# Attention decode with streamed K and V: a 31st chunk slot, smaller work tiles, and V as the stationary operand for more head pairs

## The chip, the cores and the metric

The kernel runs on one core of a Trainium2 chip. The metric is the device time of one launch in microseconds (us); three runs of the kernel before gave 1102.74, 1104.28 and 1105.88, so its median is 1104.28 us. A core has five engines that run their own instruction streams: TensorE (PE in the profile, with its weight loads shown as PEld), VectorE (DVE), ScalarE (ACT), GpSimd (POOL) and SyncE (SP). SP computes nothing here: it issues the DMAs. The engines wait for one another by semaphores.

## The reference

Two layers of the same two blocks run over 8 batch rows `b`, each with one query token: attention against a cache (A), then an MLP with two layer norms (B). Both layers read the same K and V caches, and 16 query heads share 8 K/V heads of 4096 positions by 256 elements in bf16.

```python
def _A_ref(x, k_cache, v_cache, wq, wo):
    q = (x @ wq).reshape(B, 1, 16, 256).transpose(0, 2, 1, 3)
    k = jnp.repeat(k_cache, 2, axis=1); v = jnp.repeat(v_cache, 2, axis=1)
    scores = jnp.einsum("bhqd,bhkd->bhqk", q, k) * (256 ** -0.5)
    o = jnp.einsum("bhqk,bhkd->bhqd", _softmax(scores), v)
    return o.transpose(0, 2, 1, 3).reshape(B, 1, 4096) @ wo
...
x = A_x
for _ in range(2):
    x = x + _A_ref(_layernorm(x), A_k_cache, A_v_cache, A_wq, A_wo)
    x = x + _B_ref(_layernorm(x), B_w1, B_w2, B_w3, B_w4)
```

`_B_ref` is, for one token, `x1 = x` (its shifted branch moves the only token out) followed by `x1 + gelu(layernorm(x1) @ w3) @ w4`. Rows of the batch don't mix, so one row can finish layer 0 and start layer 1 while the next row is still in layer 0.

## The kernel before

**Tiling.** The work is cut by batch row `b` and by pair `m` of K/V heads (0 to 3). A pair has two heads `s`, and a head's K (and V) is four chunks `c` of 128 partitions by 2048 elements, 0.524 MB each. A chunk lives in a slot of SBUF; there are `NSLOT = 30` slots, four to a slab. One DMA (line 444) loads one chunk, or two or four into adjacent slots that begin at a multiple of two or four (`run`, inside `schedule`); a group that finds no such run while the DMA queue is about to dry up is split in two.

**Scores.** K must be transposed first. For some chunks (`NN[m]` of each head: 1, 0, 1, 1) PE transposes into PSUM (line 810), ACT copies back (869), and PE multiplies (879). The others are transposed in blocks of 32 by DVE (891, about 1.2 us for half a chunk) from the raw slot into a second slot, and PE multiplies them (900) by a query laid out to match, in the tile `qe`. `diagonal` (602 to 633) makes that query: a DVE multiply (618), four matmuls (624), a DVE multiply (630). `qe` has two tiles, one a layer, each with room for four pairs, and one call of `diagonal` makes up to four pairs: 10 calls in layer 0 and 24 in layer 1. Softmax follows on DVE, POOL, ACT and PE (914 to 933) and leaves the probabilities in one of `NP = 4` tiles `pT` (some also in one of `NZ = 4` tiles `pN`). The tile is taken by `kpart` and given back by `vpart`.

**P*V.** `vpart` has two forms. With `still` V is the stationary operand: 16 matmuls a chunk with two moving columns (963), then a DVE reduction and multiply (966, 969). Without it p is stationary and V moves: 8 matmuls a chunk (990) into four groups of PSUM rows, which are then gathered: two ACT copies into the tile `half` (997), a matmul between them (1000), eight small matmuls (1006) and a DVE multiply (1010). Before, 17 of the 64 pairs (counting both layers and all rows) are `still`: the last pair of each row's layer 0, the first of the two pairs in each turn, and the very last pair.

**Two layers and the turn.** Row `b` runs layer 0 with all K and V streamed; pairs 1 to 3 of its K stay on chip (24 chunks, three of them parked in PSUM by `park` and put back by `unpark`, 1083). Then comes the `turn` (635 to 681): a chain of small operations that ends layer 0 (output projection 1034, `w3`, `gelu`, `w4` 587, layer norms), projects the query (`rows_`, 662), copies the rows by ACT into `qrow`, which is the tile `qe[0]` (666), transposes them (`columns`, 670) and makes layer 1's queries. During the turn SP loads V for the last pair of layer 0 and for pairs 2 and 3 of the previous row's layer 1. Then layer 1 runs on the K that stayed (pairs 1, 2, 3, no K loads), streams K of pair 0, and V; V of pairs 2 and 3 is used only in the next row's turn, so two `pT` tiles are held until then.

**Order.** The program lists all operations with priorities and costs; `Plan.schedule` plays them through a cost model and writes each engine's order. On the chip each engine runs its list in that order and waits by semaphore where an input, a buffer or a PSUM bank isn't free. SP's list is one order of loads, each of which waits for the last readers of its slot.

Of the kernel before, what the change touches and what calls it, by code (L numbers as in the profile page):

```python
# [3 lines left out]
P = 128  # L4
# [3 lines left out]
HKV = 8  # L8
# [4 lines left out]
NSLOT = 30  # L13
SLOT = 2048
AHEAD = (1, 2)
NT = 2
NS = 2
NV = 2
NP = 4
NN = (1, 0, 1, 1)  # L20
NZ = 4
# [3 lines left out]
STILL = (True, False)  # L25
# [329 lines left out]
def bass_interleave_layers__gqa_block_cached__mixer_s_mlp__decode_kernel(  # L355
# [37 lines left out]
    qe = [sb(f"qe{i}", [P, 512], bf) for i in range(2)]  # L393
    half = sb("half", [P, 1024], bf)
    pT = [sb(f"pT{i}", [P, P], bf) for i in range(NP)]
    pN = [sb(f"pN{i}", [P, 64], bf) for i in range(NZ)]

    qrow = qe[0]

    def pack(name, dt, sizes):  # L400
# [4 lines left out]
        "small32", f32, [5, 4, 4, 5, 5, 4, 8, 14, NP * 4, 8, NS * 16])  # L405
# [186 lines left out]
    Bqe = [[Buf() for _ in range(HKV // 2)] for _ in range(2)]  # L592

    def place(layer, b, m):


        return (1, b - 1) if layer == 0 and m == 0 and b in AHEAD else (layer, m)

# [3 lines left out]
    def diagonal(layer, b, m0=0, m1=4):  # L602

        k, p0 = place(layer, b, m0)
        p1 = p0 + m1 - m0
        n = 2 * (m1 - m0)
        c0 = 384 if layer else 256
        part = psT[:, c0 + 32 * m0:c0 + 32 * m1]  # L610
        qm = qe[k][:, 128 * p0:128 * p0 + 16 * n]
        bufs = [Bqe[k][m] for m in range(p0, p1)]

        def spread(e):
            src = psT[:, 64 + 8 * m0:64 + 8 * m1] if layer else qo[:, 8 * m0:8 * m1, b]
            o, i0, i1 = (qm.rearrange("p (q x) -> p q x", q=4), src.unsqueeze(1).to_broadcast([P, 4, 8 * (m1 - m0)]),
                         quarter.unsqueeze(2).to_broadcast([P, 4, 8 * (m1 - m0)]))
            return e.tensor_tensor(o, i0, i1, ALU.mult)
        dve(spread, 150 + 16 * n, [Bsel] + ([] if layer else [Bq1[b]]), bufs, [bT] if layer else [], name=f"q{layer}b{b}{m0}m")
# [7 lines left out]
        add("pe", emit, 140, bufs + [Bsel], [], [bT], name=f"q{layer}b{b}{m0}s")  # L627

        def put(e):
            return e.tensor_tensor(qe[k][:, 128 * p0:128 * p1].rearrange("p (n a h) -> p n a h", a=4, h=2),  # L630
                                   part.rearrange("p (n h) -> p n h", h=2).unsqueeze(2).to_broadcast([P, 8 * n, 4, 2]),
                                   quarter.unsqueeze(1).unsqueeze(3).to_broadcast([P, 8 * n, 4, 2]), ALU.mult)
        dve(put, 150 + 32 * n, [Bsel], bufs, [bT], name=f"q{layer}b{b}{m0}")

    def turn(b):
# [30 lines left out]
        add("act", lambda e: e.activation(qrow[:, :], psT[:, :], ACT.Copy, scale=sf[:, 2:3]), 590, [Bs["f"]], Bqe[0], [bT], name=n + "qr")  # L666

        def columns(e):
            for j in range(4):
                last = e.matmul(psT[:, 64:96].rearrange("p (r g j) -> p j r g", r=2, j=4)[:, j], qrow[:, P * j:P * j + P],  # L670
                                ident[:, :].rearrange("p (g r) -> p r g", g=4)[:, 0:2, :], start=True, stop=True)
            return last
        add("pe", columns, 300, Bqe[0] + [Bc], [], [bT], name=n + "qc", n=4)
        for ms in ((1,), (2, 3, 0)):
            if 0 in ms:
                dve(lambda e: e.tensor_copy(q2, psT[:, 64:96]), 180, [], [Bq2], [bT], name=n + "q2")
            for m in ([(1, 2)] if len(ms) == 1 else [(2, 4), (0, 1)]):
                diagonal(1, b, *m)
        plan.ops[-1].turn = "end"
        plan.turn, plan.prio = False, keep  # L680
        return ready
# [132 lines left out]
    def kpart(at, layer, b, m, kept, most=2):  # L814
# [34 lines left out]
        k, pm_ = place(layer, b, m)  # L849
        bq = Bq2 if layer else Bq1[b]  # L850
        for s in range(2):
            h = 2 * m + s
            for c in range(NCH):
# [32 lines left out]
                for t in range(2):  # L886
# [9 lines left out]
                    def score(e, u=u, c=c, t=t, s=s):  # L896
                        o = spot(psS[x])[:, :, c, t, :, s]
                        for g in range(8):
                            i = 1024 * t + g * P
                            last = e.matmul(o, slots[u.slot][:, i:i + P], qe[k][:, 128 * pm_ + 64 * s + 8 * g:128 * pm_ + 64 * s + 8 * g + 8],  # L900
# [155 lines left out]
    def K(layer, b, m, most=2):  # L1056
        at[0] += 1.0
        if layer == 0 and m < 2:
# [3 lines left out]
            elif m == 0:  # L1062
                diagonal(0, b)
# [223 lines left out]
```

## Time and profile before

| what | value |
|---|---|
| median of three runs | 1104.28 us (1102.74 to 1105.88) |
| the profiled execution | 1105.02 us, its span 1103.2 us |
| PE busy | 771.1 us, 17760 matmuls; 17807 weight loads |
| DVE busy | 746.4 us, 1417 instructions |
| ACT busy | 245.9 us |
| DMA | 446.80 MB on SP's queue, 98.2% of the 16 DMA engines' span |
| instruction loads by DMA | 139 packets, 2.28 MB |
| loads of 1, 2 and 4 chunks | 44, 218 and 88 (K and V) |
| 891, DVE transposes | 512 of 1214 ns, 598.7 us |
| 997, ACT copies into `half` | 94 of 602 ns, 56.6 us |
| 618 and 630, DVE, one pair | 192 and 289 ns |
| 630, DVE, four pairs in one | 685 ns |

A busy share is an average over stages. A row of the windows view gives, for a stretch of the span, each engine's busy time with the number of its instructions, the granted PE clock, the DMA engines' busy share and the rate in GB/s. A line of the chain of waits gives a start, a duration and the work that the end of the kernel was waiting for at that time; "issue" there is time in which PE waited for nothing that the profile shows.

### The profile page before, as it was taken

The page shows a single profiled execution, that of the slowest core. Times are in us where ns is not written, and L with a number is a line of the kernel's source. Part 1 is how long each engine was busy: PE and PEld are TensorE (multiplying, and loading weights), DVE is VectorE, ACT ScalarE, POOL GpSimd, SP SyncE. Part 2 cuts the span into 40 slices and gives each one's busy share as a digit, 9 for nine tenths or more (in the row PEclk, how much of TensorE's full clock was granted, in tenths as well). Part 3 has the DMA queues.
Part 4 walks back from the last instruction along what each step waited for, and adds up shares of the span by engine and source line. Part 5 has one row for each costly group of instructions (what it writes and reads, how often), then busy time and mean ns, then how long its engine had stood idle before and what let it go on. Part 6 is the DMA issues. An engine that isn't in the chain of part 4 may idle for free.

```text
span 1103.2 us, 38162 instructions
## 1 busy us (share of the span) xinstructions
PE 771.1 (70%) x17760; PEld 601.0 (54%) x17807; DVE 746.4 (68%) x1417; ACT 245.9 (22%) x352; POOL 69.9 (6%) x200
## 2 busy tenths in 40 slices
PE   2567576778667875778758787577766787577875
PEld 2355465466546563566536665456644566355654
DVE  3999447964696379855698458974589737885542
ACT  1033122122212131313212133121321214121310
POOL 0000001000100010000100000000000001000010
PEclk9997565565555555555555556555565556655555
DMA  9999999999999999999999999999999999999994
GB/s 348 406 420 405 396 405 409 423 408 403 425 422 411 405 427 427 422 396 417 423 425 421 401 403 426 427 418 404 416 424 424 412 405 427 425 421 400 421 423 169
DMA packets 57743, 449.24 MB, mean 407 GB/s; under 512 B 5856, under 2 KB 11888, under 8 KB 18032
## 3 DMA queue, kind: packets, MB, share of 16 engines
q1 hardware_dynamic: 57584, 446.80, 98.2%
q8 instruction: 139, 2.28, 0.8%
q14 instruction: 20, 0.16, 0.0%
HBM read 446.77 MB, written 0.01 MB: 405 GB/s over the span
## 4 chain that ended last, share of the span: by engine, by line
PE 30%; DMA 30%; DVE 23%; issue 9%; ACT 4%; POOL 0%; POOLq 0%; DVEq 0%
DMA slot<-in_A_k_cache_dram 19%; DVE slot L891 17%; DMA slot<-in_A_v_cache_dram 11%; PE psS L900 10%; PE psV L990 8%; PE psT L662 3%; ACT slot L1083 3%; PE psS L879 2%; PE psK L810 2%; PE psT L587 1%; PE psV L963 1%; ACT half L997 1%; PE psT L1034 1%; PE psT L624 1%; PE psV L1006 1%
## 5 line engine op out<-in xcount | busy, mean ns | idle before, releaser
L891 DVE STREAM_TRANSPOSE slot<-slot 128x1024 bf16<-128x1024 bf16 x512 | 598.7, 1214 | 40.3 <-DMA slot<-in_A_k_cache_dram 35.3
L900 PE MATMUL psS<-qe,slot 128*128 128x8 bf16 x6528 | 258.8, 175 | 164.5 <-DVE slot L891 121.7
L900 PEld LDWEIGHTS psS<-qe,slot 128*128 128x128 bf16 x6528 | 221.5, 104 | 236.5 <-DVE slot L891 165.7
L990 PE MATMUL psV<-slot,pT 128*2 128x256 bf16 x2448 | 154.3, 383 | 5.3 <-DMA slot<-in_A_v_cache_dram 3.6
L869 ACT COPY slot<-psK 128x1024 bf16<-128x1024 bf16 x112 | 110.8, 1027 | 168.6 <-PE psK L810 168.5
L997 ACT ACTIVATE half<-psV 128x512 bf16<-128x512 f32 x94 | 56.6, 602 | 345.6 <-PE psV L990 328.1
L810 PE MATMUL psK<-ident,slot 128*128 128x128 bf16 x896 | 104.5, 303 | 15.7 <-DMA slot<-in_A_k_cache_dram 8.1
L810 PEld LDWEIGHTS psK<-ident,slot 128*128 128x128 bf16 x896 | 88.2, 141 | 17.6 <-DMA slot<-in_A_k_cache_dram 8.8
L990 PEld LDWEIGHTS psV<-slot,pT 128*2 128x2 bf16 x2448 | 57.0, 100 | 30.5 <-issue 3.6
L914 DVE TENSOR_REDUCE small<-psS 128x4 f32<-128x128 f32 x64 | 18.4, 287 | 70.2 <-PE psS L900 69.8
L916 POOL PARTITION_ALL_REDUCE small<-small x64 | 23.9, 374 | 621.2 <-DVE small L914 621.2
L963 PE MATMUL psV<-pT,slot 128*128 128x2 bf16 x1632 | 54.2, 166 | 11.7 <-DMA slot<-in_A_v_cache_dram 11.3
L963 PEld LDWEIGHTS psV<-pT,slot 128*128 128x128 bf16 x1632 | 49.9, 105 | 20.5 <-DMA slot<-in_A_v_cache_dram 14.1
L879 PE MATMUL psS<-small,slot 128*128 128x2 bf16 x896 | 32.2, 166 | 25.8 <-issue 19.9
L879 PEld LDWEIGHTS psS<-small,slot 128*128 128x128 bf16 x896 | 28.2, 104 | 31.2 <-issue 20.6
L929 DVE STREAM_TRANSPOSE pT<-psS 128x128 bf16<-128x128 bf16 x64 | 19.2, 300 | 37.9 <-PE psS L927 37.7
L1034 PE MATMUL psT<-small,wo_sb 128*128 128x1 bf16 x1024 | 34.7, 165 | 8.1 <-DVE small L969 3.9
L921 ACT ACTIVATE pT<-psS 128x128 bf16<-128x128 f32 x64 | 18.2, 285 | 99.0 <-DVE psS L918 99.0
L932 POOL PARTITION_ALL_REDUCE small<-small x64 | 27.8, 435 | 185.0 <-DVE small L930 174.1
L879 PE MATMUL psS<-qo,slot 128*128 128x2 bf16 x768 | 28.0, 167 | 16.2 <-ACT slot L869 10.8
L990 PE MATMUL psV<-slot,pN 128*2 128x256 bf16 x560 | 38.4, 370 | 0.5 <-DMA slot<-in_A_v_cache_dram 0.4
L1034 PEld LDWEIGHTS psT<-small,wo_sb 128*128 128x128 bf16 x1024 | 30.9, 103 | 12.0 <-DVE small L1010 5.1
(148 smaller groups left out, 638.8 us busy)
## 6 DMA issues: line engine op xcount, KB each, us to landing
slot<-in_A_v_cache_dram SPq DMA_DIRECT2D x149, 1024.0 KB, 10.0
slot<-in_A_k_cache_dram SPq DMA_DIRECT2D x45, 2048.0 KB, 15.4
slot<-in_A_v_cache_dram SPq DMA_DIRECT2D x43, 2048.0 KB, 21.0
slot<-in_A_k_cache_dram SPq DMA_DIRECT2D x69, 1024.0 KB, 11.2
slot<-in_A_v_cache_dram SPq DMA_DIRECT2D x42, 512.0 KB, 6.5
wo_sb<-in_A_wo_dram SPq DMA_DIRECT2D x4, 896.0 KB, 19.2
wq_sb<-in_A_wq_dram SPq DMA_DIRECT2D x3, 1024.0 KB, 9.7
w_sb<-in_B_w_dram SPq DMA_DIRECT2D x1, 1568.0 KB, 16.4
```

The lines of the kernel that those rows point to most:

```text
L662: last = e.matmul(psT[32 * g:32 * g + 2, :], syn[:, 4 - r if k == 3 else k, 1 - r:3 - r], w, start=(r == 0 and k == 0), stop=(r == 1 and k ...
L810: last = e.transpose(tile[:, j * P:(j + 1) * P], slots[u.slot][:, o:o + P], ident[:, :])
L869: return e.copy(slots[u.slot][:, 1024 * t:1024 * t + 1024], tile)
L879: last = e.matmul(o, slots[u.slot][:, i:i + P], q, start=(cc == 0), stop=(cc == 1))
L891: return e.transpose(o, i)
L900: last = e.matmul(o, slots[u.slot][:, i:i + P], qe[k][:, 128 * pm_ + 64 * s + 8 * g:128 * pm_ + 64 * s + 8 * g + 8], start=(g == 0), stop= ...
L932: add("pool", lambda g: g.partition_all_reduce(db, rs, P, ReduceOp.add), 450, [B_["rs"]], [B_["db"]], prio=pr + 1, name=n + "db")
L963: last = e.matmul(o, slots[u.slot][:, i:i + P], w, start=(j == 0), stop=(j == 7))
L990: last = e.matmul(psV[x][32 * i:32 * i + 2, DH * s:DH * s + DH], w, slots[u.slot][:, DH * j:DH * j + DH], start=(c == 0 and k == 0), stop= ...
L997: add("act", lambda e, i=i: e.activation(part(i), psV[x][:, :], ACT.Copy, scale=1.0 if i else -1.0), 590, [], [Bhalf[i]], [bV[x]], prio=at ...
L1034: last = e.matmul(psT[:, 4 * (2 * s + i) + c:4 * (2 * s + i) + c + 1], wo_sb[:, a, d0:d0 + P], o1[b % 2][:, a:a + 1], start=(k == 0), stop ...
L1083: E = add("act", lambda e, v=v, t=t, tile=tile: e.copy(slots[v.slot][:, 1024 * t:1024 * t + 1024], tile), 1045, [], [], [bank], [v], prio= ...
```

## The change

It makes room for one more slot and changes how a few things are held:

- `NSLOT` is 31. The 31st slot is the third of its slab, so only single chunks can use it.
- `half` is gone. The gather of P*V (lines 985 to 1009) takes a free slot for its two copies, through the planner, from its first copy to its last small matmul.
- `qe` is one tile for a ring of two pairs. `diagonal` makes one pair a call; in the turn it is called for pairs 1 and 2 of layer 1, and all other calls come from `K`, just ahead of the pair's scores. A call reuses the place of the pair before last and so waits for that pair's scores.
- The query rows of the turn go into the slot in which a parked chunk's half is to be put back. That chunk's second half is put back before the copy, and its first half after `columns`.
- `NP` and `NZ` are 3. To keep that possible, `K` calls `V` of an earlier pair before it takes its own tile.
- Row sums share the statistics' columns with the maxima; the reciprocal's order after other DVE instructions is now a wait on DVE's own semaphore.
- `still` is set for both pairs in a turn, and for pair 2 of layer 0 in rows 1 to 7: 32 of the 64 pairs.

```diff
-NSLOT = 30
+NSLOT = 31
-NP = 4
+NP = 3
-NZ = 4
+NZ = 3
-STILL = (True, False)
...
-    qe = [sb(f"qe{i}", [P, 512], bf) for i in range(2)]
-    half = sb("half", [P, 1024], bf)
+    qe = sb("qe", [P, 256], bf)
...
+    def diagonal(layer, b, m):
+        k = nq[0] % 2
+        nq[0] += 1
+        qk = qe[:, 128 * k:128 * k + 128]
+        qm = qk[:, 0:32]
...
+        v, Brow = kept[b, 3][1, 0], Buf()
+        E = unpark(b, 1, ready, [1], -1.0)
+        R = add("act", lambda e: e.activation(slots[v.slot][:, 0:512], psT[:, :], ACT.Copy, scale=sf[:, 2:3]), 590, [Bs["f"]], [Brow], [bT], [v], name=n + "qr")
+        R.deps[E] = False
...
+        C = add("pe", columns, 300, [Brow, Bc], [], [bT], [v], name=n + "qc", n=4)
+        unpark(b, 1, C, [0], -0.4)
+        diagonals[1, b, 1] = diagonal(1, b, 1)
+        dve(lambda e: e.tensor_copy(q2, psT[:, 64:96]), 180, [], [Bq2], [bT], name=n + "q2")
+        diagonals[1, b, 2] = diagonal(1, b, 2)
...
-            part = lambda i: half[:, 512 * i:512 * i + 512]
+            v, Bhalf = Unit(f"{n}H", None, 0), [Buf(), Buf()]
+            part = lambda i: slots[v.slot][:, 512 * i:512 * i + 512]
...
+    def K(layer, b, m, most=2, after=None):
         at[0] += 1.0
+        prio = at[0]
+        if (layer, b, m) not in diagonals:
+            plan.prio = -0.9 if layer else prio
+            diagonals[layer, b, m] = diagonal(layer, b, m)
+        v = V(*after) if after else None
+        p = parts[layer, b, m] = kpart(prio, layer, b, m, kept[b, m] if layer else {}, most)
...
-            weave(V(1, b - 1, 2 + m, STILL[m]) if b else V(0, AHEAD[m], 0, STILL[m]))
+            weave(V(1, b - 1, 2 + m, True) if b else V(0, AHEAD[m], 0, True))
...
-                weave(ks, V(1, b, 0, most=MOST[m]) if m == first else V(0, n, m - 1, most=MOST[m]))
+                weave(*K(0, n, m, MOST[m], (1, b, 0, False, MOST[m]) if m == first else (0, n, m - 1, m == 3, MOST[m])))
```

## The prediction, made before the changed kernel was run

> **What bounds the kernel.** I read the page first, for the DMA lines and the bytes; then the windows in which the DMA rate falls; then the chain of waits through one of them.
>
> ```profile
> DMA  9999999999999999999999999999999999999994
> GB/s 348 406 420 405 396 405 409 423 408 403 425 422 411 405 427 427 422 396 417 423 425 421 401 403 426 427 418 404 416 424 424 412 405 427 425 421 400 421 423 169
> ...
> q1 hardware_dynamic: 57584, 446.80, 98.2%
> q8 instruction: 139, 2.28, 0.8%
> ```
>
> The DMA engines are busy until the last slice. 446.8 MB at the 425 GB/s of the good slices is 1051 us, so most of the span is transfer. But the rate dips below 412 once in each batch row, about every five slices. The windows lay these dips beside good stretches:
>
> ```profile
> 60.00:80.00 20.00, 13.34 (x263) 10.60 (x260) 17.82 (x23) 5.76 (x8) 1.12 (x4) 1.00 1.01 420
> 80.00:100.00 20.00, 14.95 (x331) 13.03 (x336) 19.86 (x27) 7.31 (x9) 1.45 (x4) 0.87 0.99 397
> ...
> 480.00:520.00 40.00, 31.35 (x765) 24.13 (x767) 17.52 (x72) 8.52 (x13) 2.19 (x6) 0.55 1.00 398
> 530.00:590.00 60.00, 40.12 (x801) 29.34 (x802) 51.45 (x65) 12.51 (x19) 3.88 (x11) 0.53 1.01 426
> 610.00:650.00 40.00, 30.64 (x771) 23.77 (x771) 17.05 (x71) 7.15 (x11) 2.19 (x6) 0.54 0.99 394
> ...
> 1080.00:1104.00 24.00, 12.12 (x352) 10.26 (x345) 6.16 (x40) 1.49 (x3) 0.41 (x1) 0.57 0.29 119
> ```
>
> The dips are the turns. DVE (third pair) is half idle in them, and busiest where the rate is best. The bytes that SP had issued less those that had moved (its issues in the timeline against the DMA packets) come to 2.0 to 4.6 slots in 480-490 and 500-511 us; at 545 us they are 15 to 17. So in a turn DMA is short of slots: 21 of the 30 hold K for layer 1 (24 chunks stay, three in PSUM), nine are left to stream V. The last row: 119 GB/s over 24 us is 2.86 MB, so loads end near 1087 us, and 16 us of layer ends follow, which the change does not touch. The chain through the turn near 490 us:
>
> ```profile
> 483.75 7.83 DMA slot<-in_A_v_cache_dram
> 491.62 0.60 PE psV L963 x16
> ...
> 504.86 2.72 PE psT L662 x12
> 507.60 0.70 ACT qe L666
> ...
> 510.99 1.25 PE psS L900 x48
> ...
> 515.79 0.60 ACT half L997
> 516.39 3.69 ACT slot L1083 x4
> ...
> 524.32 2.09 issue
> ...
> 530.04 3.13 issue
> ```
>
> The turn starts when the last V of layer 0 lands (491.6) and frees K slots only from the scores at 510. The "issue" pieces are PE waiting for instructions: PE ran 649 + 649 of them in 484 to 514 us and 557 + 555 in 514 to 544, and 35567 in all arrive in 139 packets, 256 each. Ten such packets moved in 484 to 546, one per 6.2 us: PE there gets 256 instructions per 6 us and no more.
>
> **What can be won.** Against the 420 GB/s of ordinary two-chunk loads, the turns lose width times (1 - rate/420). 140-190 at 406: 1.7; 240-280 at 401: 1.8; 350-390 at 406: 1.3; 480-520 at 398: 2.1; 610-650 at 394: 2.5; 740-780 at 400: 1.9; 870-910 and 1000-1040 at 405: 1.4 each. Sum 14.1 us; with 80-100 at 397 (1.1 us) 15.2 us. That is all that a better supply of slots can give.
>
> **The change, part by part.**
>
> *The 31st slot.* It costs SBUF alone: 4096 bytes a partition against 1536 from `qe`, 2048 from `half`, 256 and 128 from `pT` and `pN`, 80 from statistics (48 bytes more in all). It is worth one chunk more in flight, 0.524 MB at 425 GB/s = 1.23 us of cover per drought. A turn has two: before the last softmax of layer 0 (480-490 us, 376 GB/s) and before the first scores of layer 1 (510-520, 401). Bounds 0 and 15.2 us. Interpolating, 3.3 slots in flight give about 390 and 5.5 give 419, so one more brings back 45%; that a full queue in the first drought also lands the V that starts the turn sooner speaks for more. I take 60%: **-9.1 us**. The slot takes single chunks only, which suits the DVE transposes' targets, so I don't cut further.
>
> *V stationary for 15 more pairs.* Per pair 64 matmuls, 1 and 8 for the gather become 128: 55 more with their weight loads, 110 instructions. PE time hardly differs (990: 0.98 us for 16, two chunks; 963: 1.01 us for 32, two chunks). ACT loses 30 copies of 0.60 us, of which the one at 515.79 stands on the chain ahead of the put-back; but 6 to 8 slots are then in flight, so I count nothing. DVE gains 15 reductions of 194 ns. The cost is instruction supply: 110/256 x 6 us = 2.6 us per pair where PE is at its limit. For pair 2 of layer 0 (470-482 us; packets 8 to 10 us apart) it hides. For the turn's second pair it stands ahead of the scores that free slots. Bounds 0 (PE has waits of its own from 504 to 510, for the copy at 507.6 and the transposes) and 8 x 2.6 = 20.6 us. Near the lower end, because the wait at 507 absorbs most: 0.4 us a turn, **+3.0 us**. The extra bytes, 15 x 110 + 30 calls of `diagonal` x 8 = 1890 instructions, are 0.12 MB: **+0.3 us**.
>
> [...]
>
> *One pair a call of `diagonal`.* 34 calls become 64, each 192 + 289 ns on DVE and four matmuls. Before, rows 618 and 630 sum to 7.9 + 13.7 = 21.6 us; after, 64 x 0.481 = 30.8: 9.2 us more DVE, 1.2 a batch row. In the turn there is one call fewer. Behind a call's second multiply stand that pair's DVE transposes, and it waits for the scores of two pairs earlier. In streaming stretches 13 to 20 slots (16 us and more) are in flight while DVE is full: hidden, 0. Uncovered: 12 us with the reductions.
>
> *Gather in a slot.* 32 gathers hold one slot from the first 0.60 us copy to the last small matmul, about 2.5 us (482.9 to 485.1 before). ACT waits for a free slot with the softmax exponentials (921) queued behind. None is in the turn now, and elsewhere the queue is deep: 0; uncovered, 32 x 1.23 = 39 us at the very most.
>
> *Rows in a waiting slot.* ACT runs one put-back (1.0 us), the rows, the other put-back. The rows waited for PE (`L662`) anyway, 0.88 us idle before 507.6; the late half is needed only for pair 3. 0, within 1 us a turn either way.
>
> *Three p tiles.* Two are held across the row, so the streaming pairs share one: a pair's exponential (ACT) waits for the previous pair's last V product. At 483 us V of pair 2 was done at 482.8 (its copy starts 482.91) and the exponential came at 485.54: 2.7 us to spare. With four-chunk loads V lands one load, 4.9 us, after K and needs 2.5 us; K needs 6 to 8 transposes of 1.2 us and 1.5 more: margin 1 to 3.7 us. 0; if gone, 1 us at some 40 pairs, mostly under the deep queue.
>
> Shared statistics order what was ordered: 0.
>
> **Sum.** -9.1 + 3.0 + 0.3 = -5.8 us. The profiled execution took 1105.0 (span 1103.2 and 1.8 around it), 0.7 above the median: 1104.3 - 5.8 = **1098.5 us**.
>
> **Rivals.**
> 1. *PE is not delayed and the droughts close*: 9.1 to 14 us less, 1090 to 1095; centre 1093. For it: PE idles 504 to 510 anyway. Against: the issue pieces. 0.20. [...]
> 2. *The slot is not used where it counts*: pairs of chunks need aligned places, the 31st has none; fewer tiles eat the rest. 1102 to 1107, centre 1104. For it: most turn loads are two chunks. Against: the DVE transposes' targets are taken singly, and then leave a pair elsewhere. 0.15.
> 3. *Instruction supply decides (slower)*: the 110 instructions push the scores of layer 1's first pair by a whole 2.6 us. From 1.23 us on the new slot no longer covers it. Then the second drought stays and grows by 1.4 us a turn: 8 x 1.4 = +11, the first drought's relief -4.5: 1111. For it: ten packets in 62 us, at the limit. Against: PE's waits in that place. 0.12.
> 4. *The shared p tile or the query ring (slower)*: exponentials late by 1 us at 40 pairs, a tenth covered less than I think, or half of the 12 us of DVE shows: +4 to +10 less a part of the gain, 1108. 0.08.
>
> Forecast 0.45, its own range 1094.5 to 1101. What a measurement of this kernel can tell from no change is 0.3%, 3.3 us. Faster: forecast and rival 1, 0.65; same: rival 2, 0.15; slower: 0.20. The range goes from 1090 to 1108.
>
> **What would show it.** Turn windows above 406 GB/s with 4 or more slots in flight; loads ending near 1081; 64 copies on the gather, 4096 matmuls with V stationary, 64 rows each of the two query multiplies, some 146 instruction packets. Wrong if the turn windows stay near 400, if issue pieces grow ahead of layer 1's first scores, or if the exponential waits for V products.

## The result, and the profile after

The changed kernel took 1115.11 us (median of five runs, 1113.15 to 1117.56), the kernel before 1104.43 on the same chip (five runs, 1102.74 to 1107.21). The ratio is 1.0093, its 95% interval 1.0070 to 1.0116: slower by 10.7 us, where 5.8 us less was forecast. The profiled execution took 1117.56 us with a span of 1115.8, 12.6 us above the span before.

The page of the changed kernel first: its rate in 40 slices, its queues, the chain by engine, and three rows of its groups.

```profile
GB/s 357 406 420 417 395 390 369 423 417 398 420 423 412 412 404 428 421 414 388 405 425 420 409 391 427 427 418 386 368 426 426 418 399 393 426 421 411 388 423 192
...
q1 hardware_dynamic: 56576, 446.80, 97.5%
q8 instruction: 146, 2.39, 0.8%
...
PE 31%; DVE 26%; DMA 22%; issue 12%; ACT 4%; SPq 4%; POOL 1%; DVEq 0%; POOLq 0%; ACTq 0%
...
L883 DVE STREAM_TRANSPOSE slot<-slot 128x1024 bf16<-128x1024 bf16 x512 | 605.2, 1217 | 28.9 <-DMA slot<-in_A_k_cache_dram 21.7
...
L956 PE MATMUL psV<-pT,slot 128*128 128x2 bf16 x2960 | 96.3, 165 | 17.0 <-DMA slot<-in_A_v_cache_dram 14.6
...
L991 ACT ACTIVATE slot<-psV 128x512 bf16<-128x512 f32 x64 | 38.2, 597 | 203.3 <-PE psV L983 191.8
```

The change did what its text says: 64 gather copies instead of 94, 2960 + 1136 = 4096 matmuls with V stationary, 146 instruction packets, the numbers forecast. The same 446.8 MB are loaded. What is worse is the rate in single slices (369, 368, 386) and the share of "issue" in the chain, 12% where it was 9%.

The windows of the turn near 495 us say where. Each row is a stretch: 20 us ahead of the turn, the turn up to the third put-back of a parked chunk, and 25 us behind it. First the changed kernel, then the one before.

```profile
core 0: us, PE busy (x) PEld busy (x) DVE busy (x) ACT busy (x) POOL busy (x), PEclk, DMA share, GB/s
478.00:498.00 20.00, 14.32 (x381) 13.47 (x379) 8.87 (x16) 2.21 (x3) 1.02 (x3) 0.50 1.01 410
498.00:524.00 26.00, 18.81 (x530) 14.60 (x527) 8.88 (x56) 3.10 (x5) 0.80 (x2) 0.50 1.00 404
524.00:549.00 25.00, 19.74 (x509) 17.17 (x510) 17.52 (x37) 8.84 (x13) 3.48 (x10) 0.52 0.95 380
...
791.00:816.00 25.00, 18.12 (x478) 15.90 (x481) 18.29 (x35) 8.29 (x11) 3.27 (x9) 0.50 0.91 373
```

```profile
473.70:493.70 20.00, 13.99 (x342) 12.57 (x344) 9.05 (x15) 3.40 (x5) 1.02 (x3) 0.59 1.00 386
493.70:516.30 22.60, 19.69 (x493) 13.92 (x490) 8.30 (x54) 3.34 (x5) 0.80 (x2) 0.58 1.01 411
516.30:541.30 25.00, 17.16 (x459) 15.27 (x461) 17.53 (x29) 8.80 (x13) 2.89 (x8) 0.50 1.01 426
```

Ahead of the turn the rate rose from 386 to 410: the first drought did close here. The turn is 3.4 us longer, at a lower rate, and the stretch behind it fell from 426 to 380. A DMA share of 1.00 stands in most of these rows, those at 386 and 404 too: there the loss shows in the rate alone, and only in the rows at 380 and 373 GB/s in the share as well (0.95, 0.91).

The chain of waits of the changed kernel through the same turn (start, duration, work):

```profile
513.69 1.04 PE psS L892 x39
514.73 1.69 issue
516.42 0.41 PE psS L892 x9
516.82 0.84 PE psV L956 x32
...
519.59 0.41 PE psS L892 x15
520.00 3.18 issue
523.18 0.63 PE psS L892 x17
523.83 3.77 ACT slot L1079 x4
```

PE has layer 1's first scores at hand and twice waits for instructions, 1.69 and 3.18 us: instruction packets start at 514.15 and 520.74, and PE goes on 2.3 and 2.4 us after them. The put-back comes at 523.83, 28.7 us after V landed at 495.12; before it was 24.8 us (491.62 to 516.39). SP's next load waits up to 9.5 us for these scores:

```profile
SPq L440 <- PE psS L892: 26.8, 9, 9.5
SPq L440 <- PE psV L956: 11.5, 4, 5.3
```

(The queue's waits in 498 to 549 us: total, times, longest.) In 526 to 530 us only some 1.5 slots were in flight on average; before, at the same place behind the turn (517 to 529), about 6.

To add this up I counted every load packet at the time that it takes in the good stretches (0.611 us for 16 KB) and took what is missing to 16 busy engines as **lost transfer**, in us. Its sums over the eight turns:

```
                ahead (20 us)  turn   behind (25 us)  whole kernel
before               6.6        6.7        1.1            19.5
after                3.3       11.8       15.5            32.7
```

The difference of 13.2 us is the 12.6 us of span (the loads themselves come out 0.7 us less). Loads end at 1101.9, and 13.9 us of layer ends follow, 14.0 before: nothing was lost there.

### The profile page after: what moved, and what is told of

Same layout as the page of the kernel before. It is cut to its first block, busy times and chain, and to the rows that moved or that the text cites. A ratio compares the mean times of both kernels' runs of the same rounds, so it can differ in the third digit from the quotient of the medians.

```text
span 1115.8 us, 40203 instructions
## 1 busy us (share of the span) xinstructions
PE 785.0 (70%) x18752; PEld 627.7 (56%) x18752; DVE 755.2 (68%) x1492; ACT 229.3 (21%) x322; POOL 70.0 (6%) x200
## 4 chain that ended last, share of the span: by engine, by line
PE 31%; DVE 26%; DMA 22%; issue 12%; ACT 4%; SPq 4%; POOL 1%; DVEq 0%; POOLq 0%; ACTq 0%
DVE slot L883 20%; DMA slot<-in_A_k_cache_dram 15%; PE psS L892 10%; DMA slot<-in_A_v_cache_dram 7%; PE psV L983 6%; PE psV L956 5%; SPq L421 3%; PE psT L652 3%; ACT slot L1079 2%; PE psS L871 2%; PE psK L802 2%; PE psT L583 1%; SPq L440 1%; ACT slot L991 1%; PE psT L1027 1%
## 5 line engine op out<-in xcount | busy, mean ns | idle before, releaser
L883 DVE STREAM_TRANSPOSE slot<-slot 128x1024 bf16<-128x1024 bf16 x512 | 605.2, 1217 | 28.9 <-DMA slot<-in_A_k_cache_dram 21.7
L892 PE MATMUL psS<-qe,slot 128*128 128x8 bf16 x6528 | 251.1, 175 | 175.8 <-DVE slot L883 113.6
L892 PEld LDWEIGHTS psS<-qe,slot 128*128 128x128 bf16 x6528 | 215.1, 105 | 241.8 <-DVE slot L883 161.7
L983 PE MATMUL psV<-slot,pT 128*2 128x256 bf16 x1784 | 115.4, 404 | 1.6 <-issue 1.0
L802 PE MATMUL psK<-ident,slot 128*128 128x128 bf16 x896 | 102.5, 298 | 11.8 <-issue 4.4
L956 PE MATMUL psV<-pT,slot 128*128 128x2 bf16 x2960 | 96.3, 165 | 17.0 <-DMA slot<-in_A_v_cache_dram 14.6
L956 PEld LDWEIGHTS psV<-pT,slot 128*128 128x128 bf16 x2960 | 88.9, 104 | 24.1 <-DMA slot<-in_A_v_cache_dram 16.4
L802 PEld LDWEIGHTS psK<-ident,slot 128*128 128x128 bf16 x896 | 86.2, 138 | 18.8 <-ACT slot L1079 7.4
L991 ACT ACTIVATE slot<-psV 128x512 bf16<-128x512 f32 x64 | 38.2, 597 | 203.3 <-PE psV L983 191.8
L913 ACT ACTIVATE pT<-psS 128x128 bf16<-128x128 f32 x64 | 18.2, 284 | 204.7 <-DVE psS L910 157.6
L983 PEld LDWEIGHTS psV<-slot,pT 128*2 128x2 bf16 x1784 | 44.4, 106 | 23.4 <-issue 1.9
L956 PE MATMUL psV<-pN,slot 128*128 128x2 bf16 x1136 | 40.1, 165 | 16.2 <-issue 7.6
L956 PEld LDWEIGHTS psV<-pN,slot 128*128 128x128 bf16 x1136 | 35.2, 103 | 27.2 <-issue 15.2
L871 PE MATMUL psS<-small,slot 128*128 128x2 bf16 x896 | 32.2, 167 | 16.3 <-issue 10.8
L871 PEld LDWEIGHTS psS<-small,slot 128*128 128x128 bf16 x896 | 28.9, 105 | 21.5 <-issue 13.7
## 6 DMA issues: line engine op xcount, KB each, us to landing
slot<-in_A_v_cache_dram SPq DMA_DIRECT2D x160, 1024.0 KB, 10.5
```

Source lines behind the costliest of these rows:

```text
L802: last = e.transpose(tile[:, j * P:(j + 1) * P], slots[u.slot][:, o:o + P], ident[:, :])
L871: last = e.matmul(o, slots[u.slot][:, i:i + P], q, start=(cc == 0), stop=(cc == 1))
L883: return e.transpose(o, i)
L892: last = e.matmul(o, slots[u.slot][:, i:i + P], qe[:, 128 * k + 64 * s + 8 * g:128 * k + 64 * s + 8 * g + 8], start=(g == 0), stop=(g == 7))
L956: last = e.matmul(o, slots[u.slot][:, i:i + P], w, start=(j == 0), stop=(j == 7))
L983: last = e.matmul(psV[x][32 * i:32 * i + 2, DH * s:DH * s + DH], w, slots[u.slot][:, DH * j:DH * j + DH], start=(c == 0 and k == 0), stop= ...
```

## The experiments

Eighteen kernels, each beside the kernel before on the same chip. The table gives medians, ratios to the kernel before with their 95% intervals, and the lost transfer of the profiled execution of each. The ratios are what compares: the kernel before took 1105.92 to 1106.87 us beside the eighteen. Differences of some 4 us between two profiles tell nothing: `n1_noise` lost 10.9 us ahead of its turns, before 6.6, and its time is the same.

| run | us | ratio [95%] | ahead | turn | behind |
|---|---|---|---|---|---|
| before | 1104.43 | 1 | 6.6 | 6.7 | 1.1 |
| after | 1115.11 | 1.0093 [1.0070, 1.0116] | 3.3 | 11.8 | 15.5 |
| e1_turn | 1114.03 | 1.0079 [1.0052, 1.0105] | 10.3 | 16.4 | 1.0 |
| e2_pair2 | 1116.49 | 1.0111 [1.0078, 1.0144] | 6.0 | 18.8 | 3.3 |
| e3_both | 1118.91 | 1.0119 [1.0096, 1.0142] | 7.0 | 23.0 | 2.4 |
| e4_30 | 1120.82 | 1.0134 [1.0114, 1.0154] | 11.4 | 10.1 | 11.0 |
| e9_np4 | 1120.65 | 1.0125 [1.0100, 1.0150] | 12.0 | 7.1 | 9.3 |
| e12_ring4 | 1120.01 | 1.0120 [1.0099, 1.0141] | 11.9 | 10.2 | 10.5 |
| e10_half | 1120.89 | 1.0132 [1.0095, 1.0169] | 10.4 | 6.4 | 11.3 |
| e13_all | 1113.59 | 1.0066 [1.0043, 1.0089] | 8.2 | 13.7 | 0.4 |
| n1_noise | 1106.22 | 0.9998 [0.9987, 1.0010] | 10.9 | 7.0 | 1.1 |
| p1_bpad | 1115.53 | 1.0089 [1.0065, 1.0112] | 7.5 | 14.5 | 1.2 |
| p5_b256 | 1105.87 | 0.9996 [0.9983, 1.0010] | 7.9 | 5.5 | 0.5 |
| p2_apad | 1119.07 | 1.0108 [1.0059, 1.0157] | 10.5 | 18.2 | 4.9 |
| p3_e3pad | 1114.49 | 1.0076 [1.0056, 1.0096] | 7.5 | 16.1 | 1.4 |
| p4_e13pad | 1111.30 | 1.0048 [1.0030, 1.0066] | 10.1 | 10.2 | 2.1 |
| e5_bstill | 1117.48 | 1.0098 [1.0071, 1.0125] | 10.1 | 11.4 | 8.5 |
| e6_bnone | 1108.82 | 1.0020 [1.0003, 1.0037] | 7.4 | 11.9 | 0.8 |
| e7_bn | 1112.00 | 1.0054 [1.0035, 1.0074] | 9.1 | 6.5 | 3.3 |
| b7_bn | 1107.26 | 1.0011 [0.9999, 1.0023] | 11.8 | 3.6 | 0.8 |

### First round: undo V stationary, undo the slot

`e1_turn` makes the turn's second pair moving again, `e2_pair2` pair 2 of layer 0, `e3_both` both (17 stationary pairs, as before); `e4_30` keeps everything but the slot.

```diff
 e1, e3: -  weave(V(1, b - 1, 2 + m, True) if b else V(0, AHEAD[m], 0, True))
         +  weave(V(1, b - 1, 2 + m, m == 0) if b else V(0, AHEAD[m], 0, m == 0))
 e2, e3: -  ... else (0, n, m - 1, m == 3, MOST[m])))
         +  ... else (0, n, m - 1, False, MOST[m])))
 e4:     -NSLOT = 31
         +NSLOT = 30
```

> The changed kernel with the second pair of each turn put back to moving V (64 matmuls and a gather instead of 128), all else kept. Theory I (PE's instruction supply: the 110 extra instructions of that pair stand ahead of layer 1's first scores and of all that frees K slots): the hole after the turn shrinks to what it was before; 1103 to 1107 us against 1115.1 of the changed kernel, the longest issue pieces ahead of the put-back under 2 us. Theory II (the ring of two queries and the three p tiles delay layer 1): 1112 to 1116, the hole stays.

> The changed kernel with pair 2 of layer 0 in rows 1 to 7 put back to moving V, all else kept. That pair stands ahead of the turn. Theory I: instruction loads are 7 to 8 us apart there, so there is slack and nothing is gained; 1113 to 1116. If the supply is short already ahead of the turn, up to 2.6 us in each of seven rows: 1098 to 1108. Theory II: 1113 to 1116.

> The changed kernel with V stationary in the same 17 pairs as before: the 31st slot, the gather in a slot, the rings and three p tiles alone. Theory I: as the first run of this call or a little faster; 1098 to 1106. Theory II: 1112 to 1116, since all that it blames is still there.

> The changed kernel with 30 slots, all else kept: the worth of the slot by itself. From the prediction's term (9 us less by the slot) 1122 to 1126. If the slot only fills the drought ahead of the turn, where the rate rose, and the hole after the turn doesn't depend on it: 1118 to 1121. If the slot is worth nothing: 1115.

In the changed kernel the slot is worth something: without it the ratio goes from 1.0093 to 1.0134, so about 0.4% or 4.5 us, and the loss ahead of the turns from 3.3 to 11.4. It does more than add a chunk in flight. Fewer groups are split: the kernel with 30 slots loads V 42 times by single chunks, as the kernel before does, the one with 31 slots 16 times (first `e4_30`, then after).

```profile
slot<-in_A_v_cache_dram SPq DMA_DIRECT2D x42, 512.0 KB, 7.2
```

```profile
slot<-in_A_v_cache_dram SPq DMA_DIRECT2D x16, 512.0 KB, 7.4
```

Neither secures the gain: `e1_turn` has 31 slots and the same 16, and loses 10.3 ahead of its turns. Undoing V stationary did not bring the time back: -1.5 us by ratio for `e1`, +2 and +3 for `e2` and `e3`, intervals overlapping. But the loss moved. With the second pair of the turn moving, the stretch behind the turns is whole again (1.0, against 15.5), and the turns themselves lose more (16.4 and 23.0). A part undone in a changed program was not the mirror of the part done alone, and something besides the added instructions was at work in the turn.

### Second round: the tiles, and how much a mere reordering does

`e9_np4` gives the 30-slot kernel four tiles `pT` and `pN` (three before), `e12_ring4` a ring of four queries, `e13_all` both, `half` as a tile of its own and the old 17 stationary pairs. `n1_noise` is the kernel before with the cost of a DVE transpose put at 1150 instead of 1135 in the planner, which reorders some PE and DVE work.

```diff
 e9, e13:      -NP = 3   +NP = 4   -NZ = 3   +NZ = 4
 e12, e13:     -    qe = sb("qe", [P, 256], bf)
               +    qe = sb("qe", [P, 512], bf)
               -        k = nq[0] % 2
               +        k = nq[0] % 4
               ...
 n1 (before):  -E = add("dve", square, 1135, ...
               +E = add("dve", square, 1150, ...
```

> The changed kernel with 30 slots and with four tiles of p and of its copy again; to be read against the changed kernel with 30 slots (1120.8 us), which differs in those tiles alone. Theory II for the p tiles (an exponential waits for the previous pair's last V product, and scores and V behind it): 1108 to 1114. Theory III (PE's instruction supply in the turn decides, by where the ends of the 256-instruction blocks fall in the order that the planner happens to make): no systematic gain, 1115 to 1123, and the loss of a run follows the issue stalls in its turns.

> The changed kernel with 30 slots and a ring of four pairs' queries instead of two, so that a query needn't wait for the scores of the pair before last. Against 1120.8 us with the ring of two. Theory II for the ring: 1108 to 1114. Theory III: 1115 to 1123.

> The changed kernel with 30 slots, four p tiles, a ring of four queries, the gather in a tile of its own, and V stationary in the 17 pairs of before. What is left of the change is one pair a call of the query layout (two calls in the turn), the rows in a waiting slot, and the shared statistics. If the rings, tiles and the gather cost the time: 1103 to 1107. If the split calls or the rows cost it, or the order that the planner makes is worse by itself: 1112 to 1120.

> The kernel before with one number of the planner's cost model changed, a DVE transpose at 1150 instead of 1135 ns: no operation, tile or slot differs, only the order that the planner writes. Theory III: the time moves by 3 to 12 us, since the turns' block ends fall elsewhere. If the order is robust: 1103 to 1107.

The p tiles and the ring cost nothing that can be measured (1.0125 and 1.0120 against 1.0134 for `e4_30`). That deserves a closer reading, since in the changed kernel ACT's waits show a row that the kernel before does not have (total, times, longest):

```profile
ACT pT L913 <- PE psV L983: 47.1, 8, 6.5
```

47 us of an exponential waiting for a V product, and no time that can be measured in it: with four tiles (`e9_np4`) the row is gone and the time is the same. The one reordering tried does nothing either (`n1_noise`, where theory III asked for 3 to 12 us); but it starts its turns at nearly the same places of a block as the kernel before, so it is no test of the place. Yet `e13_all`, with little of the change left, is still 0.66% slower, and its loss sits in the turns (13.7) while the stretch behind them is whole (0.4).

### Third round: the place in a block of instructions

PE's instructions arrive in packets of 256 (35567 in 139 packets before, 37504 in 146 in the changed kernel). If PE is short of them in the turn, what it has at hand when a turn starts would depend on where in a block it stands: the number of instructions executed up to the turn, modulo 256. Counted as twice the weight loads in the trace, the kernel before runs 4340 = 17 x 256 - 12 from one turn to the next (from the third turn on), and its turns all start at 80 to 154. `e3_both` (4372 = 17 x 256 + 20) starts at 106, 202, 2, 22 and so on up to 102. Most of the texts below put the same places 10 to 50 higher. The third round shifts this by idle transposes at the program's start, each two instructions, with no other change.

```diff
+    def pad(e):
+        for _ in range(98):
+            last = e.transpose(psX[:, 0:P], ident[:, :], ident[:, :])
+        return last
+    add("pe", pad, 0.0, [Bc], [], [bX], prio=-2.0, name="pad", n=0)
```

(98 in `p1_bpad` and `p2_apad`, 43 in `p3_e3pad`, 48 in `p4_e13pad`, 128 in `p5_b256`.)

> The kernel before with 98 transposes of the identity into a free tile at the program's start (196 TensorE instructions more, nothing else changed; output the same). They shift where the boundaries of TensorE's 256-instruction blocks fall in the eight turns: the instructions executed ahead of a turn, modulo 256, go from 100 to 165 to about 40 to 105. Theory of the phase (TensorE gets 256 instructions per about 6.2 us under a saturated DMA, so a turn that starts late in a block has fewer instructions at hand): the turns stall as in the runs with altered counts, 1112 to 1122 us, and the issue stalls in the turns go from 8 us to over 16. Rival (the count of instructions in the turn and the planner's order decide, not the phase): the pads cost at most 2 us at the start, 1104 to 1107.

> The kernel after with the same 98 transposes at the start. Theory of the phase: phases go to about 85 to 151, the turns themselves lose less, but the turns still have some 1050 to 1165 instructions where before had 970, so the hole behind the turn stays: 1108 to 1115. Rival (phase does not matter): 1114 to 1118, the hole of 15 us behind the turns and 12 us in them as it is.

> V stationary in the old 17 pairs alone (1118.9 us), with 43 transposes (86 instructions) at the start. Theory of the phase: phases go from 213, 14, 34, ... 94, 114 to 43, 100, 120, ... 180, 200, where enough is buffered, and the turns' loss of 23 us of DMA time falls to under 10: 1104 to 1109. Rival (the phase does not matter): 1117 to 1121.

> 30 slots, four p tiles, a ring of four queries, the old 17 pairs (1113.6 us), with 48 transposes (96 instructions) at the start. Theory of the phase: phases go from 189, 250, 19, ... 119 to 29, 90, 115, ... 215, the turns' loss of 13.7 us falls to about 6: 1104 to 1108. Rival (the phase does not matter; what is left of the change, the program order of K and V and the rows in a waiting slot, costs the 7 us): 1112 to 1115.

> The kernel before with 128 transposes of the identity at the start: 256 TensorE instructions, a whole block, against 196 in the run that took 1115.5 us. Theory of the phase (what counts is the number of instructions ahead of a turn modulo 256): the turns start at the same 100 to 165 as in the kernel before, issue stalls in the turns 7 to 10 us, 1104 to 1108 us. Rival (the padding itself, its time or its reads at the start, disturbs the run): as with 196 or worse, 1112 to 1118, stalls in the turns near 20 us.

The pair `p1` and `p5` is the cleanest result of the study. 196 idle instructions, the first that PE runs (98 transposes, 7.6 us busy in a start where PE waits for its first loads, 3.8 us for `wqt_sb` in the kernel before), make the old kernel 0.89% slower; 256 of them, more work, cost nothing (0.9996). The rest of the program and its order are the same, so it is the place modulo 256. PE's groups in the first 6 us of the turn near 760 us show it (matmuls of `w3` and `w4` in the layer's end; busy, mean ns, then idle and what ended it). First `p1`, then `p5`, whose row numbers are those of before plus 5:

```profile
L569 PE MATMUL psT<-small,w3t_sb 128*128 128x1 bf16 x14 | 1.6, 165 | 1.2 <-issue 1.2
...
L592 PE MATMUL psT<-small,w_sb 128*128 128x1 bf16 x19 | 0.7, 166 | 0.4 <-DVE small L582 0.4
```

```profile
L569 PE MATMUL psT<-small,w3t_sb 128*128 128x1 bf16 x14 | 1.6, 165 | 0.0
L592 PE MATMUL psT<-small,w_sb 128*128 128x1 bf16 x29 | 0.9, 166 | 0.6 <-DVE small L582 0.6
```

In `p1` there is a stall of 1.2 us in the first small matmuls, and 6 us into the turn ten fewer of the `w4` matmuls are done. `p5` has its stall of that size right behind these 6 us; `p1` has a second one, in the middle of 16 matmuls of V. From the two chains, `p1` first:

```profile
763.97 1.20 issue
...
769.23 0.08 PE psV L968 x3
769.31 2.08 issue
771.38 0.48 PE psV L968 x13
```

```profile
761.23 0.93 PE psT L592 x29
762.16 1.21 issue
763.37 0.87 PE psT L592 x27
```

The windows of the same two turns (up to the third put-back), `p1` and then `p5`:

```profile
762.10:786.70 24.60, 19.76 (x489) 13.68 (x486) 8.41 (x55) 3.44 (x6) 0.80 (x2) 0.50 0.99 393
```

```profile
756.40:778.60 22.20, 19.28 (x492) 13.62 (x490) 8.31 (x54) 3.29 (x5) 0.79 (x2) 0.58 1.01 403
```

The same work, 2.4 us longer, at 393 instead of 403 GB/s. The granted clock differs too (0.50 and 0.58), but it is not the cause: what PE does without a stall takes the same time in both chains (32 matmuls of V 0.94 us, two stretches of the query projection 1.45 and 2.23 us), and the kernel before has a clock of 0.50 in its turn at 757 us, at 405 GB/s. The mean over turns 2 to 8 went from 22.1 us (before) to 23.5, the issue stalls of over 0.3 us in all eight from 9.0 to 21.7 us; in `p5` they are 21.7 and 5.7.

What these stalls are, all twenty traces show together. After the first instruction packet PE stands still for over 0.8 us without a cause in the profile 574 times. In 568 of them it goes on 2.2 to 2.7 us after an instruction packet starts, and they all stand at one place of a block: 178 to 188 instructions in early in a kernel, falling slowly to 134 to 144 at its end. So they are waits for the next block. What the start of a turn in its block decides is how far into the turn the first such crossing falls: 14 to 52 instructions in turns 2 to 8 of before and `p5`, which stall 0.2 to 1.4 us each, and 74 to 159 in the turns of `p1`, which stall 1.3 to 3.7 us.

What is late is V, as far as a correlation shows. A stalled PE does the turn's V products later, and these free the slots of the next loads (SP's 11.5 us of waits for `psV` L956 above). Counting V chunks multiplied in the first 4 us of a turn (by their weight loads, mean of turns 2 to 8): 3.5 before, 3.4 in `p5`, 2.4 in `p1`, 1.2 in `e3_both`, 2.0 in `p3`. Over the twenty kernels of the table this count and the loss in the turns correlate at -0.87.

On the altered kernels the shift did less than the theory asked. `p3` gained 0.43% (expected 0.9 to 1.3%), `p4` 0.18% with overlapping intervals, and `p2` nothing (ratio up 0.15%, within its wide interval): three times outside both ranges that were expected. The place in the block is one cause, not the whole.

### Last rounds: V stationary alone, the planner told, the other end

`e5_bstill` changes one constant of the kernel before, `e6_bnone` the same constant the other way, `e7_bn` and `b7_bn` one constant of the planner after and before, `e10_half` gives the gather its own tile in the 30-slot kernel.

```diff
 e5:      -STILL = (True, False)
          +STILL = (True, True)
 e6:      -STILL = (True, False)
          +STILL = (False, False)
 e7, b7:  -BLOCK, BLOCK_0, BLOCK_NS = 128, 84, 4500.0
          +BLOCK, BLOCK_0, BLOCK_NS = 128, 84, 6200.0
 e10:     +    half = sb("half", [P, 1024], bf)
          ...
          -            part = lambda i: slots[v.slot][:, 512 * i:512 * i + 512]
          +            part = lambda i: half[:, 512 * i:512 * i + 512]
          ...
```

> The kernel before with one constant changed: V stationary in both pairs of the turn and in all pairs near it, as the kernel after has it; 30 slots, two tiles of p, separate tiles for the gather as before. If the added instructions are what made the kernel after slower: 1114 to 1122 us, holes in and behind the turns of 20 us or more together (7.8 before). If it is the slot or the sharing of tiles that did it: 1104 to 1109. The forecast of record had +3.0 for this part: 1107 to 1109 by it.

> The kernel before with V moving in all pairs: 880 TensorE instructions fewer in all, some 55 fewer in each step of a turn's pairs. By the program the turns 2 to 8 begin at 12, 190, 68, 202, 80, 214 and 92 instructions into a block (before: 138, 170, 158, 146, 134, 122, 110). Theory of count and place: the turns at 190 to 214 lose at most 1 us of transfer each with issue stalls under 1 us, those at 12 and 68 to 92 lose 1.5 to 3 us with stalls over 2; in all 1103 to 1111 us. Rival (V stationary is what keeps the turn short, and its instructions cost nothing in the kernel before): every turn longer by 1 us or more, 1112 to 1120, whatever the place.

> The kernel after with one constant of its planner changed: a block of 128 matmuls is reckoned at 6.2 us instead of 4.5, as the packets of instructions come in the trace. If the holes stem from work ordered for a TensorE that gets its instructions faster than it does, the planner now spreads or drops V stationary where it does not fit: 1104 to 1111 us, the hole behind the turns under 8 us (15.5). If the supply bounds the turn whatever the order: 1112 to 1118.

> The kernel before with the same constant of its planner, 6.2 us a block instead of 4.5. If the planner's reckoning matters by itself: 1098 to 1104 us. If the kernel before has its turns in a lucky place modulo 256 and any new order moves them: 1107 to 1116 us, with the issue stalls in the turns above 14 us (8.1).

> The kernel after with 30 slots and a tile of its own for the gather of P*V, all else as after (V stationary in all pairs). With the gather in a slot and 30 slots it was 1120.8 us; the kernel before with V stationary in all pairs was 1117.5. If the gather in a slot costs about what the added slot gives: 1115 to 1118. If it costs nothing, as forecast: 1119.5 to 1122, and what is left between 1117.5 and 1120.8 lies in the order of K and V and the query rows.

Two of these texts say more than the constant does: `STILL` governs the two pairs in a turn alone. `e5` adds the eight second pairs of the turns (25 stationary pairs, not the 32 of after; it has four tiles of p, not two), and `e6` takes out the eight first ones (9 stay).

**V stationary by itself.** In the kernel before, with its 30 slots and all its tiles, it costs 0.98%, 10.8 us, for eight pairs: about 1.4 us a turn. Its chain through the turn that starts at 767.8 us:

```profile
787.78 1.50 PE psS L900 x56
789.28 0.36 PE psV L963 x14
789.64 3.46 issue
793.11 0.64 PE psV L963 x18
793.75 0.45 PE psS L900 x16
794.20 0.02 issue
794.22 3.77 ACT slot L1083 x4
```

The chain of `p5` (as before, second pair moving) through its turn that starts at 756.4:

```profile
775.55 1.59 PE psS L905 x56
777.14 0.98 PE psV L995 x13
778.12 0.02 issue
778.14 0.60 ACT half L1002
778.74 3.69 ACT slot L1088 x4
```

Put-back 26.4 us into the turn against 22.3. The moving V stands there for 0.98 us of PE and 0.60 us of ACT; the stationary V for 3.46 us of waiting in the middle of its 32 matmuls. It loses in the stretch behind the turns too (8.5 against 1.1).

The edit also moves the turns to other places in the block, and the trace tells the two apart. The first crossing comes 48 to 254 instructions into `e5`'s turns, and at every place they stall 2.7 to 4.9 us. At 48 and 51 it is 4.4 and 3.6 us, where turns of before at 49 and 52 stall 0.7 and 1.2. So here it is the added instructions, and not the place.

How near a turn stands to the supply is seen in the counts (PE instructions and weight loads from the turn's first reduction to the third put-back, means of turns 2 to 8):

```
             instructions  turn us   per us
e6_bnone          879        22.6      38.8    (six of the seven: 22.0 to 22.6)
before            969        22.1      43.9
after            1056        24.4      43.4
e5_bstill        1098        24.7      44.5
```

A turn that hardly stalls takes some 22 us, and PE then gets some 44 instructions per us: 41 from packets of 256 that start 6.2 us apart, the rest, by estimate, from what was at hand. 44 x 22 = 968, so the kernel before stands near that balance. In `e5` and after the added instructions lengthen the turn at about that rate, and below it (`e6`) nothing is gained. It is no law: `e2_pair2` and `p2_apad` run about 1050 instructions in turns of 22.8 and 22.5 us and lose their transfer inside the turn (18.8 and 18.2), and `e13_all` and `p1_bpad` take 23.6 and 23.5 us for about 969.

**The planner told 6.2 us a block** takes the changed kernel from 1.0093 to 1.0054 and the loss behind its turns from 15.5 to 3.3 us; its 1112.0 us is still 1 us above the range expected for a cure by order. In the kernel before, the turns lose least of all (3.6), but smaller loads (76 of one chunk instead of 44) and the stretch ahead of the turns (11.8) go with no gain. Its 1107.26 us lies in the range that its text gives for turns moved to worse places, but not for that reason: its turns start within 16 instructions of the old places, and their stalls of over 0.3 us come to 5.9 us.

**The gather in a slot** costs nothing that can be measured: 1.0132 with its own tile, 1.0134 without, at intervals of 2 to 4 us either way.

**The place, within one run.** In `e6` the turns 3, 5 and 7 start at 190 to 214 of a block, meet their first crossing 190 to 234 instructions later and have no issue stall over 0.3 us. Of the others, turn 4 (crossing 96 in) stalls 3.37 us and takes 25.0, turns 2 and 6 (161 and 73 in) stall 0.66 and 1.02, and turn 8 (51 in) not at all. That fits `p1` and `p5`; but the loss in the turns (11.9) is about as large in either group, so it is not made by the stalls alone.

No version beat the kernel before; `p5` and `n1_noise` are level with it.

## Why the prediction was wrong

**The step that failed** is "V stationary for 15 more pairs", +3.0 us, of which the turn's pairs were 0.4 us each "because the wait at 507 absorbs most". Done alone, the turn's pairs cost 10.8 us, 1.4 us each. The working had the right price in hand: 110 instructions at 6 us per 256 are 2.6 us, and the upper bound of 20.6 holds the measured cost. The choice inside the bounds was wrong. A wait of PE for its data at 507 us was taken for room in which missing instructions can arrive. The traces show little at hand: when an instruction packet starts, PE has at most 272 instructions left, about one block (median near 140; instructions run, set against packets moved), and the turns of `e5_bstill` stall wherever the crossings fall. Dividing 969 instructions by 22 us and setting that beside 256 per 6.2 us would have shown that hardly any room was left. Crossings of a block stand in the chains above with 1.2 to 3.5 us each, and the block of 256 instructions that the sum used is borne out by the 35567 in 139 packets, the places of the stalls, and `p1` and `p5`.

**The slot** had the right sign at half the size in the changed kernel: about 4.5 us against 9.1. The drought ahead of the turn, which I expected to close, was smaller in that kernel's profile (6.6 to 3.3); with the same 31 slots and other orders or places it was 6.0 to 10.5 (`e2`, `e3`, `e1`, `p2`), so the 3.3 is not the slot's alone. And with 17 stationary pairs the kernel with 31 slots is the slower one (`e3_both` 1.0119, `e13_all` 1.0066; with shifted turns 1.0076 and 1.0048). Those two differ in tiles and places as well, so what the slot is worth by itself stays open.

**The terms at nothing.** The p tiles, the query ring and the gather in a slot each cost nothing within the intervals. For the p tiles that is luck: the margin of 1 to 3.7 us on which the 0 rested was not there (waits of up to 6.5 us, 47.1 in all), and they cost nothing all the same. The rows in a waiting slot, one pair a call of `diagonal`, and the order of K ahead of V were never tried by themselves. `e13_all`, which holds these, the shared statistics, 30 slots and 17 stationary pairs, is 0.66% slower, and 0.48% with its turns moved to other places in the block: some 5 us of the change that no term of the sum holds. What of it is the place and what a cost of these edits stays open.

**In sum**, by ratios: slot -0.4%, V stationary in the turn +1.0%, the rest +0.5 to +0.7% (`p4_e13pad`, `e13_all`): 1.1 to 1.3%, against 0.93% measured. The sum is a rough one, since `e1` to `e3` show that the parts do not add: with the pairs moving again, program counts change, the places in the block with them, and the turns lose what the stretch behind them gains.

**The rivals.** Rival 3, instruction supply, is what happened, at 1111 where 1115.1 was measured; that it came so near is in part luck, since the 5 us that no term holds are not in it either, and the stated range ended at 1108, short of it. Its relief of the first drought (-4.5) measured -3.3 in the one profile; its growth of 1.4 us a turn measured 2.4 (the turn and the stretch behind it, 8 turns, 27.3 - 7.8 = 19.5 us). It was given 0.12, since PE's own waits were set against it. Rivals 1 and 4 fell: PE is delayed, and the shared tiles do not count; rival 2 fell in the changed kernel, where the slot counts. Two of the signs named in advance pointed right: issue pieces ahead of layer 1's first scores grew, and loads ended at 1101.9 where 1081 would have shown the forecast true. The third, an exponential that waits for V products, came too and meant nothing. The layer ends behind the last load, put at 16 us, are 14.

## What to carry to other kernels

Where an unrolled stretch runs at the rate at which instructions come, count them: the number in the stretch over its time, against the spacing of the instruction packets. If the two are level, a form with more and shorter instructions can cost its count, as in `e5_bstill` (129 more and 2.6 us more in a turn), however idle the engine looks by its busy share (70% here). And before a part of one per cent is credited to an edit, shift the program by some idle instructions, once by a part of a block and once by a whole one: if the first moves the time and the second doesn't, a difference of that size may be the place and not the edit.

## What the runs showed of the hardware

- 196 idle TensorE instructions at the start changed the time of this 1.1 ms kernel by 0.89% [0.65, 1.12] (`p1_bpad`), 256 by -0.04% [-0.17, 0.10] (`p5_b256`).
- In and around a turn, instruction packets of 16 KB started 6.0 to 6.4 us apart (medians of the runs), in kernels of 879 to 1103 instructions a turn alike, while one packet was mostly under way for 0.9 to 1.1 us. Single gaps were shorter, down to 3.4 us (`e2_pair2`, 374 us), so 256 per 6 us was no fixed limit here.
- Counted over the twenty traces, a packet started 3.3 us (median) after PE entered the last block that it had, where loads moved at over 300 GB/s, and 0.5 us after it in the 28 cases where they moved at under 100; a stalled PE ran its instructions 2.4 us (median) after that start. 3.3 and 2.4 make 5.7 of the 6 us; what the 3.3 us consist of was not shown.
- In most windows in and around a turn the busy share of the DMA engines read 0.99 to 1.02, at rates from 382 to 428 GB/s. A packet took longer where the rate was lower (8 KB in 337 ns on average in 765 to 791 us of the changed kernel, at 382 GB/s and a share of 0.99; in 315 in 60 to 80 us of the kernel before, at 420 and 1.01), so the share did not show the loss.
